# Loading wo in 1 MB pieces through the K/V ring and doing the output projection at the end of a decode kernel

## The chip, the cores and the metric

One core of one Trainium2 chip. The metric is the device time of one execution in microseconds (us). Every run told here counts as fast: none is over 1.5% above the fastest run of its kernel. The granted clock is the share of full speed at which the chip let TensorE run. Names of engines in the profile: PE is TensorE, PEld its weight loads, DVE VectorE, ACT ScalarE, POOL GpSimd, SP the engine that issues the DMAs.

## The reference

One decode step: a token (batch 2, width 1024) attends over a cache of 32 heads x 16384 keys x 128, and the result is mixed by a gate with a small MLP.

```python
q = (x @ wq).reshape(B, 1, H, Dh)                # B=2, D=1024, H=32, Dh=128
scores = einsum("bhqd,bhkd->bhqk", q, k_cache) * Dh ** -0.5   # Sk = 16384
o = einsum("bhqk,bhkd->bhqd", softmax(scores), v_cache)
a = o.reshape(B, 1, H * Dh) @ wo                 # wo: 4096 x 1024, 8 MB in bf16
out = g * a + (1 - g) * mlp(x)                   # mlp cut: layernorm, w1..w4
```

K and V are 537 MB, all weights 36 MB, everything in bf16.

## The kernel before

A planner appends operations to one queue per engine; every engine runs its queue in program order and waits on semaphores for the others. A "pair" is one (head, batch): 4 K pieces and 4 V pieces of 1 MB each, which pass through a ring of 16 slots. Odd K pieces get their scores on DVE (two products with the query, four reductions), even ones on TensorE (transposes, then matmuls with the query). V pieces follow K with a lag of 5 pieces.

```python
stream = []
for n in range(NKP):                     # 256 K pieces
    stream.append(("K", n))
    if n >= LAG:                         # LAG = 5
        stream.append(("V", n - LAG))
...
def kpath(n):                            # the last TAILP = 6 K pieces all on TensorE
    return "p" if n >= NKP - TAILP else "pd"[n % 2]

def softmax(i):                          # called once all scores of pair i are planned
    mx_tk[i] = DVE  max of the scores along the free axis
    poolmax_tk[i] = POOL partition_all_reduce(max)
    nbias_tk[i] = POOL tensor_scalar( * -scale)
    exp_tk[i] = ACT exp -> ptile, with row sums
    pooladd_tk[i] = POOL partition_all_reduce(add) of the row sums

def do_A(h):                             # output projection of one head, 8 small matmuls
    waits = [fin_tk[h * Bsz + b] for b in range(Bsz)] + [wo_loaded[h]]
    for nt_i in range(KT):               # KT = 8: 128x128 of wo against 128x2
        P.op("pe", matmul(AT_ps[...], lhsT=wor[...], rhs=otb[...]))   # AT_ps adds up over heads

def finish(i):                           # after the last V piece of pair i
    ...                                  # 1/sum on DVE; O4_ps copied to od (ACT)
    ...                                  # 4 matmuls sum od into one column; ACT scales it into otb
    if b == Bsz - 1:
        pending_A.append(h)

for (kind, n) in stream:
    if kind == "V" and b == 0 and pc == 0:       # one wo load of 256 KB per head, 3 buffers
        wo_loaded[h] = P.dma("sp", wor[...] <- A_wo[h * 128:(h + 1) * 128, :])
    ...
    if kind == "K":
        make_qrep(i), make_w(i)          # ACT copies of the query, at the pair's first K piece
        ...                              # scores, by path
        if pending_A:
            do_A(pending_A.pop(0))
    else:
        ...                              # 8 matmuls 128x4 against 128x512 per V piece, into O4_ps
```

## Time and profile before

The first three runs took 2071.6, 2074.2 and 2088.2 us.

| stage of the profiled run (2075.1 us) | us |
|---|---|
| weights and MLP, to the first K work on TensorE | 83 |
| result of the 4th pair's POOL max to that of the 62nd (58 pairs) | 1788.9, or 30.84 per pair |
| from there to the end | 88.4 |
| TensorE / DVE / DMA busy over the span | 60% / 56% / 70% |

No engine is near full, so the question is what waits for what. The page's chain that ended last, by engine:

```profile
DVE 48%; issue 34%; PE 10%; ACT 4%; POOL 2%; SPq 1%; DMA 1%; POOLq 0%; DVEq 0%
```

"issue" is time in which the chain's engine waited for nothing that the profile shows. The same chain in order of time, for one pair (start in us, duration in us, what):

```profile
1001.31 4.51 DVE prd L676 x2
...
1015.07 4.61 DVE ssb L685 x4
...
1020.18 0.37 POOL st L472
1020.55 0.06 POOLq L475 x2
...
1020.62 10.39 issue
1031.01 0.27 POOL st L475
```

Between the first and the second line lie one more round of reductions (4.61 us) and one more of products (4.50 us). DVE works through its two K pieces, takes the max, and then the chain stands for 10.39 us. The POOL all-reduce of the max over the 128 partitions (L472) starts just ahead of that; its record is 0.37 us long. Behind it POOL's sequencer runs two MODIFY_POOL_CONFIG instructions (`POOLq L475 x2`), and only 10.4 us later does the next POOL instruction start, the scaling of the max by L475.

I call the time from the start of the max's all-reduce to the start of the next POOL instruction (L475) the **POOL wait**; where the texts below speak of the all-reduce or of the POOL round trip, they mean this. After it the exp runs on ACT, then ACT's copy of the next query, then DVE again. No TensorE work is in the list.

The projection in the timeline of that same stretch (start, duration, engine, line, operation; in brackets the idle time before it and what ended it):

```profile
1040.44 0.35 PE L562 MATMUL ps<-otb,wor 128*128 128x2 bf16 x8 [0.36 <-ACT otb L593]
...
1049.78 0.28 ACT L536 ACTIVATE ssb<-ps 128x32 f32<-128x32 f32 x2 [0.52 <-PE ps L527]
...
1050.55 0.29 DVE L470 TENSOR_REDUCE st<-ssb 128x1 f32<-128x128 f32 x1
```

The eight matmuls take 0.35 us. TensorE's scores of this pair are in place at 1050.06 us, and DVE, which had its own reductions until 1050.42, starts the max at 1050.55.

The end of the timeline, from the second last exp on:

```profile
2019.49 0.40 ACT L477 ACTIVATE ptile<-ssb,st 128x128 bf16<-128x128 f32 x1 [8.31 <-POOL st L475]
...
2049.20 0.29 DVE L470 TENSOR_REDUCE st<-ssb 128x1 f32<-128x128 f32 x1 [37.53 <-ACT ssb L536]
...
2057.67 0.40 ACT L477 ACTIVATE ptile<-ssb,st 128x128 bf16<-128x128 f32 x1 [8.61 <-POOL st L475]
...
2060.49 8.87 PE L710 MATMUL ps<-ring,ptile 128*4 128x512 bf16 x32
```

29.7 us from the second last exp to the last max (here DVE waits for scores from TensorE), then the last POOL wait, then 17.4 us from the last exp to the end (2075.1), 8.9 of them the last pair's P·V.

### The profile page before, as it was taken

Reading aid. Unit: us, or ns where it says so; the run is one execution under the profiler, and the core shown is the slowest. Engines: PE = TensorE matmul, PEld = TensorE weight load, DVE = VectorE, ACT = ScalarE, POOL = GpSimd, SP = SyncE. Lnnn points to the kernel's source line nnn. Section 1 sums busy time; section 2 is a strip of 40 time slices with the busy share of each in tenths; the row PEclk is TensorE's granted clock in tenths of the full one; section 3 lists DMA queues with packets and bytes.
Section 4 is the critical chain, followed back from the end, with each engine's and each line's share of the span. In section 5 each row is a group of like instructions: output and inputs, shape, how many; then the busy total and the mean of one; then the engine's idle time right before and its main releaser. Section 6 shows DMA issues by size and latency. Waiting matters only on the chain.

```text
span 2075.1 us, 17839 instructions
## 1 busy us (share of the span) xinstructions
PE 1250.5 (60%) x7119; PEld 628.1 (30%) x7119; DVE 1166.0 (56%) x917; ACT 667.0 (32%) x1177; POOL 75.1 (4%) x213
## 2 busy tenths in 40 slices
PE   2565565665575575566566556557556656656557
PEld 2322232332232232232233223223223223323223
DVE  1365565575575566566566557557556656656620
ACT  1232233232333333333333223233333333323333
POOL 1000000000000000000000000000000000000000
PEclk9977877888888888888888888888888888778888
DMA  9996766776776776676686676677667667667650
GB/s 384 408 400 248 303 250 262 309 271 256 298 280 260 281 304 256 267 314 250 260 323 259 260 307 268 259 293 295 254 276 303 255 261 306 254 266 306 254 200 1
DMA packets 86612, 573.72 MB, mean 276 GB/s; under 512 B 9216, under 2 KB 9216, under 8 KB 19968
## 3 DMA queue, kind: packets, MB, share of 16 engines
q1 hardware_dynamic: 86528, 572.57, 70.0%
q8 instruction: 56, 0.92, 0.2%
q14 instruction: 28, 0.23, 0.0%
HBM read 572.53 MB, written 0.00 MB: 276 GB/s over the span
## 4 chain that ended last, share of the span: by engine, by line
DVE 48%; issue 34%; PE 10%; ACT 4%; POOL 2%; SPq 1%; DMA 1%; POOLq 0%; DVEq 0%
DVE ssb L685 23%; DVE prd L676 23%; PE ps L710 4%; PE ps L514 3%; ACT ptile L477 2%; PE ps L643 1%; POOL st L472 1%; SPq L242 1%; ACT ktr L653 1%; POOL st L475 1%; DVE st L470 1%; DMA ring<-in_B_w_dram 1%; PE ps L314 1%; PE ps L588 1%; ACT qrep L573 0%
## 5 line engine op out<-in xcount | busy, mean ns | idle before, releaser
L676 DVE TENSOR_TENSOR prd<-ring,qrep 128x2048 f32<-128x2048 bf16 x250 | 561.7, 2288 | 735.2 <-ACT wbuf L491 728.8
L514 PE MATMUL ps<-ktr,wbuf 128*32 128x512 bf16 x1048 | 347.8, 439 | 684.1 <-ACT ktr L653 684.1
L685 DVE TENSOR_REDUCE ssb<-prd 128x8 f32<-128x1024 f32 x500 | 574.8, 1212 | 4.3
L653 ACT ACTIVATE ktr<-ps 128x1024 bf16<-128x1024 bf16 x524 | 500.3, 1024 | 186.8 <-PE ps L643 186.4
L710 PE MATMUL ps<-ring,ptile 128*4 128x512 bf16 x2048 | 529.7, 405 | 15.3 <-ACT ptile L477 15.3
L514 PEld LDWEIGHTS ps<-ktr,wbuf 128*32 128x32 bf16 x1048 | 82.2, 99 | 812.2 <-ACT ktr L653 736.1
L643 PE MATMUL ps<-ident_f,ring 128*128 128x128 f32 x2096 | 317.6, 298 | 0.0
L643 PEld LDWEIGHTS ps<-ident_f,ring 128*128 128x128 f32 x2096 | 244.0, 150 | 115.9 <-issue 111.6
L710 PEld LDWEIGHTS ps<-ring,ptile 128*4 128x4 bf16 x2048 | 181.1, 93 | 303.8 <-issue 114.1
L477 ACT ACTIVATE ptile<-ssb,st 128x128 bf16<-128x128 f32 x64 | 25.7, 401 | 766.6 <-POOL st L475 766.6
L585 ACT ACTIVATE od<-ps 4x512 f32<-4x512 f32 x64 | 37.6, 587 | 151.7 <-PE ps L710 151.7
L588 PEld LDWEIGHTS ps<-ident_f,od 4*128 4x128 f32 x512 | 62.4, 188 | 36.3 <-ACT od L585 36.3
L588 PE MATMUL ps<-ident_f,od 4*128 4x1 f32 x512 | 67.9, 249 | 9.0 <-ACT od L585 9.0
L522 ACT ACTIVATE stsb<-ps 32x512 f32<-32x512 f32 x64 | 37.6, 587 | 104.6 <-PE ps L514 104.6
L472 POOL PARTITION_ALL_REDUCE st<-st x64 | 25.5, 399 | 901.6 <-DVE st L582 842.0
L470 DVE TENSOR_REDUCE st<-ssb 128x1 f32<-128x128 f32 x64 | 18.3, 286 | 68.3 <-ACT ssb L536 61.0
L527 PE MATMUL ps<-ident_f,stsb 32*128 32x32 f32 x256 | 27.5, 227 | 43.7 <-ACT stsb L522 43.7
L527 PEld LDWEIGHTS ps<-ident_f,stsb 32*128 32x128 f32 x256 | 20.4, 136 | 75.3 <-ACT stsb L522 75.3
L593 ACT ACTIVATE otb<-ps,st 128x1 bf16<-128x1 f32 x64 | 16.9, 264 | 80.9 <-PE ps L588 79.6
L475 POOL TENSOR_SCALAR st<-st 128x1 f32<-128x1 f32 x64 | 18.3, 286 | 661.1 <-issue 661.1
L480 POOL PARTITION_ALL_REDUCE st<-st x64 | 25.7, 401 | 389.6 <-issue 212.3
L536 ACT ACTIVATE ssb<-ps 128x32 f32<-128x32 f32 x131 | 18.6, 195 | 33.2 <-PE ps L527 33.2
(83 smaller groups left out, 172.4 us busy)
## 6 DMA issues: line engine op xcount, KB each, us to landing
ring<-in_A_k_cache_dram SPq DMA_DIRECT2D x256, 1024.0 KB, 7.2
ring<-in_A_v_cache_dram SPq DMA_DIRECT2D x256, 1024.0 KB, 7.4
ring<-in_B_w_dram SPq DMA_DIRECT2D x11, 1024.0 KB, 19.9
ring<-in_A_wq_dram SPq DMA_DIRECT2D x8, 1024.0 KB, 12.0
wor<-in_A_wo_dram SPq DMA_DIRECT2D x32, 256.0 KB, 7.5
ring<-in_B_w_dram SPq DMA_DIRECT2D x8, 896.0 KB, 15.3
x<-in_A_x_dram SPq DMA_DIRECT2D x1, 4.0 KB, 1.5
gw<-in_gate_w_dram SPq DMA_DIRECT2D x1, 2.0 KB
```

The costliest lines, as they stand in the source:

```text
L470: mx_tk[i] = P.op("dve", lambda e: e.tensor_reduce(stc(j, M_P), S_sb(j), AX.X, ALU.max), part_tk[i] + [prev(poolmax_tk, i, NPB)])
L472: poolmax_tk[i] = P.op("pool", lambda e: e.partition_all_reduce(stc(j, GMAX), stc(j, M_P), channels=128, reduce_op=RED.max), [mx_tk[i], pr ...
L475: nbias_tk[i] = P.op("pool", lambda e: e.tensor_scalar(stc(j, NBIAS), stc(j, GMAX), -scale, None, ALU.mult), [poolmax_tk[i], prev(exp_tk, ...
L477: exp_tk[i] = P.op("act", lambda e: e.activation(P_ap(j, 0, NCH), S_sb(j), ACTF.Exp, bias=stc(j, NBIAS), scale=scale, accum_out=stc(j, L_P ...
L514: e.matmul(ST_ps(i), lhsT=l, rhs=r, start=st_, stop=sp_)),
L527: tk = P.op("pe", (lambda e, t4=t4: e.transpose(Sp_ps[:, t4 * 32:(t4 + 1) * 32], stj[:, t4 * 128:(t4 + 1) * 128], ident_f[0:32, 0:32])), ( ...
L588: osum_tk[i] = P.op("pe", (lambda e, m=m: e.matmul(oT_ps, lhsT=odj[:, m * 128:(m + 1) * 128], rhs=ident_f[0:VG, m:m + 1], start=(m == 0), ...
L643: e.transpose(o, a, ident_f[:])),
L653: evac_tk[gn] = P.op("act", lambda e, o=o_pl, a=a_pl: e.activation(o, a, ACTF.Copy), ew)
L676: last = P.op(eng, (lambda e, o3=o3, i3=i3, qb3=qb3: e.tensor_tensor(o3, i3, qb3, ALU.mult)), ([ring_loaded[jp], qrep_tk[i]] + wfree) if q ...
L685: red = P.op("dve", (lambda e, o=o, a=a: e.tensor_reduce(o, a, AX.X, ALU.add)), ([last, prev(exp_tk, i, NPB)]) if g_ == 0 else ())
L710: e.matmul(O4_ps, lhsT=l, rhs=rr, start=st_, stop=sp_)),
```

## The change

The intent: take the 32 small wo loads and the 32 small projection groups out of the middle of the kernel. wo comes in 8 loads of 1 MB (4 heads each) through slots of the K/V ring near the end of the stream, and each piece is multiplied in one run of 32 matmuls. With it comes a shorter last pair: its P·V is done with V as the stationary operand (128 matmuls of one column) straight into the layout that the projection needs.

```diff
--- before.py
+++ after.py
@@ -61,7 +61,9 @@
     cfg = dict(cfg or {})
     NSLOT = cfg.get("NSLOT", 16)
     NKT = cfg.get("NKT", 4)
-    NWO = cfg.get("NWO", 3)
+    WOGAP = cfg.get("WOGAP", 2)
+    WTAIL = cfg.get("WTAIL", 2)
+    LASTBT = cfg.get("LASTBT", 1)
     NQ = cfg.get("NQ", 32)
     QKLAG = cfg.get("QKLAG", 2)
     EVAC = cfg.get("EVAC", "a")
@@ -71,6 +73,7 @@
     PSPLIT = cfg.get("PSPLIT", 4)
     NPRD2 = cfg.get("NPRD2", 2)
     TAILP = cfg.get("TAILP", 6)
+    TAILK = cfg.get("TAILK", 0)
     NT = 3
     VG = 4
 
@@ -103,7 +106,6 @@
 
     ring = nc.alloc_sbuf_tensor("ring", [128, NSLOT * PE_ELEMS], BF16)
     ktr = nc.alloc_sbuf_tensor("ktr", [128, NKT * 1024], BF16)
-    wor = nc.alloc_sbuf_tensor("wor", [128, NWO * D], BF16)
     ident_bf = nc.alloc_sbuf_tensor("ident_bf", [128, 128], BF16)
     ident_f = nc.alloc_sbuf_tensor("ident_f", [128, 128], F32)
     qsb = nc.alloc_sbuf_tensor("qsb", [128, NPAIR + NQ], BF16)
@@ -116,7 +118,7 @@
     ptile = nc.alloc_sbuf_tensor("ptile", [128, NPB * NCH], BF16)
     ssb = nc.alloc_sbuf_tensor("ssb", [128, NPB * NCH], F32)
     st = nc.alloc_sbuf_tensor("st", [128, NPB * 8], F32)
-    otb = nc.alloc_sbuf_tensor("otb", [128, 2 * Bsz], BF16)
+    otb = nc.alloc_sbuf_tensor("otb", [128, NPAIR], BF16)
     od = nc.alloc_sbuf_tensor("od", [VG, NPB * VG * 128], F32)
     prd = nc.alloc_sbuf_tensor("prd", [128, PE_ELEMS], F32)
     prd2 = (nc.alloc_sbuf_tensor("prd2", [128, NPRD2 * PE_ELEMS], F32)
@@ -177,6 +179,7 @@
     msel_ps = bank_f(1, 0, 4 * NPAIR)
     qrep_ps = bank_f(7, 0, 128)
     O4_ps = ps[0:VG, 5 * 512: 6 * 512]
+    Obt_ps = ps[:, 5 * 512: 5 * 512 + 1]
     AT_ps = bank_f(6, 0, W)
     QT_ps = bank_f(0, 0, NPAIR)
     xTp = bank_b(7, 0, W)
@@ -219,8 +222,6 @@
     P = _Plan(nc)
     slot_sem = [nc.alloc_semaphore("slot%d" % s) for s in range(NSLOT)]
     slot_uses = [0] * NSLOT
-    wo_sem = [nc.alloc_semaphore("wo%d" % s) for s in range(NWO)]
-    wo_uses = [0] * NWO
     misc_sem = nc.alloc_semaphore("misc_dma")
     misc_sem2 = nc.alloc_semaphore("misc_dma2")
     out_sem = nc.alloc_semaphore("out_dma")
@@ -409,13 +410,38 @@
         return cache[b, h, pc * PKEYS:(pc + 1) * PKEYS, :].rearrange("(p r) d -> p (r d)", p=128)
 
     NKP = NPAIR * NPC
+    HPP = max(1, min(H, PE_ELEMS // D))
+    NWOP = -(-H // HPP)
     stream = []
+    nv = 0
     for n in range(NKP):
         stream.append(("K", n))
-        if n >= LAG:
-            stream.append(("V", n - LAG))
-    for n in range(max(0, NKP - LAG), NKP):
-        stream.append(("V", n))
+        if n >= LAG and n < NKP - TAILK:
+            stream.append(("V", nv))
+            nv += 1
+    while nv < NKP:
+        stream.append(("V", nv))
+        nv += 1
+    n_tail = min(WTAIL, NWOP)
+    n_before = NWOP - n_tail
+    pos = len(stream)
+    inserts = []
+    for k_ in range(n_before):
+        pos = max(0, pos - WOGAP)
+        inserts.append(pos)
+    inserts.reverse()
+    for gw, pos in reversed(list(enumerate(inserts))):
+        stream.insert(pos, ("W", gw))
+    for gw in range(n_before, NWOP):
+        stream.append(("W", gw))
+    seen_v = set()
+    for (kind, n) in stream:
+        if kind == "V":
+            seen_v.add(n)
+        elif kind == "W":
+            need_pairs = range(n * HPP * Bsz, min(NPAIR, (n + 1) * HPP * Bsz))
+            early = [i_ for i_ in need_pairs if (i_ * NPC + NPC - 1) not in seen_v]
+            assert not early or n >= NWOP - n_tail - 1, (n, early)
 
     def kpath(n):
         if n >= NKP - TAILP:
@@ -550,20 +576,25 @@
         while len(pending_qk) > keep:
             issue_qk(pending_qk.pop(0))
 
-    def do_A(h):
-        hs = h % 2
-        s = h % NWO
-        waits = [fin_tk[h * Bsz + b] for b in range(Bsz)] + [wo_loaded[h]]
+    def wo_piece(gw):
+        h0 = gw * HPP
+        nh = min(HPP, H - h0)
+        src = A_wo[h0 * 128:(h0 + nh) * 128, :].rearrange("(t p) n -> p t n", p=128)
+        dv = (lambda s_, nh=nh: slot_ap(s_, 0, nh * D).rearrange("p (t n) -> p t n", t=nh))
+        jp, s_ = ring_dma(src, dst_view=dv)
         last = None
-        for nt_i in range(KT):
-            last = P.op("pe", (lambda e, o=AT_ps[:, nt_i * Bsz:(nt_i + 1) * Bsz],
-                               l=wor[:, s * D + nt_i * 128: s * D + (nt_i + 1) * 128],
-                               r=otb[:, hs * Bsz:(hs + 1) * Bsz], st_=(h == 0 and nt_i == 0), sp_=(h == H - 1):
-                               e.matmul(o, lhsT=l, rhs=r, start=st_, stop=sp_, skip_group_check=True)),
-                        waits if nt_i == 0 else (), track=(nt_i == KT - 1))
-        A_tk[h] = last
-
-    pending_A = []
+        for hh in range(nh):
+            h = h0 + hh
+            waits = [ring_loaded[jp]] + [fin_tk[h * Bsz + b] for b in range(Bsz)]
+            for nt_i in range(KT):
+                last = P.op("pe", (lambda e, o=AT_ps[:, nt_i * Bsz:(nt_i + 1) * Bsz],
+                                   l=slot_ap(s_, hh * D + nt_i * 128, hh * D + (nt_i + 1) * 128),
+                                   r=otb[:, h * Bsz:(h + 1) * Bsz], st_=(h == 0 and nt_i == 0), sp_=(h == H - 1):
+                                   e.matmul(o, lhsT=l, rhs=r, start=st_, stop=sp_, skip_group_check=True)),
+                            waits if nt_i == 0 else (), track=(nt_i == KT - 1))
+            A_tk[h] = last
+        ring_free[jp] = last
+
 
     def make_qrep(i):
         j = i % NPB
@@ -581,6 +612,11 @@
         hs = h % 2
         rl_tk[i] = P.op("dve", lambda e: e.reciprocal(stc(j, RL), stc(j, LSUM)),
                         [pooladd_tk[i], prev(fin_tk, i, NPB)])
+        if LASTBT and i == NPAIR - 1:
+            fin_tk[i] = P.op("act", (lambda e, o=otb[:, i:i + 1]:
+                                     e.activation(o, Obt_ps, ACTF.Copy, scale=stc(j, RL))),
+                             [pvlast_tk[i], rl_tk[i]])
+            return
         odj = od[:, j * VG * 128:(j + 1) * VG * 128]
         ocopy_tk[i] = P.op("act", lambda e: e.activation(odj, O4_ps, ACTF.Copy),
                            [pvlast_tk[i], prev(osum_tk, i, NPB)])
@@ -589,12 +625,10 @@
                 oT_ps, lhsT=odj[:, m * 128:(m + 1) * 128], rhs=ident_f[0:VG, m:m + 1],
                 start=(m == 0), stop=(m == VG - 1))),
                 ([ocopy_tk[i], t_identf] + list(b7_read)) if m == 0 else (), track=(m == VG - 1))
-        fin_tk[i] = P.op("act", (lambda e, o=otb[:, hs * Bsz + b: hs * Bsz + b + 1]:
+        fin_tk[i] = P.op("act", (lambda e, o=otb[:, i:i + 1]:
                                  e.activation(o, oT_ps, ACTF.Copy, scale=stc(j, RL))),
-                         [osum_tk[i], rl_tk[i], prev(A_tk, h, 2)])
+                         [osum_tk[i], rl_tk[i]])
         b7_read[:] = [fin_tk[i]]
-        if b == Bsz - 1:
-            pending_A.append(h)
 
     def cprime(c):
         pcq, r = c // R, c % R
@@ -605,15 +639,12 @@
         return ap.rearrange("p (r d) -> p r d", d=DH)
 
     for (kind, n) in stream:
+        if kind == "W":
+            wo_piece(n)
+            continue
         i, pc = n // NPC, n % NPC
         h, b = i // Bsz, i % Bsz
         j = i % NPB
-        if kind == "V" and b == 0 and pc == 0:
-            s = h % NWO
-            wo_uses[s] += 1
-            wo_loaded[h] = P.dma("sp", (lambda e, s=s, h=h: e.dma_start(
-                wor[:, s * D:(s + 1) * D], A_wo[h * 128:(h + 1) * 128, :])), wo_sem[s], 16 * wo_uses[s],
-                [prev(A_tk, h, NWO)])
         cache = A_k_cache if kind == "K" else A_v_cache
         jp, s = ring_dma(kv_src(cache, i, pc))
         if kind == "K":
@@ -689,14 +720,21 @@
                 else:
                     prd2_free[pb] = red
                 add_part(i, red)
-            if pending_A:
-                do_A(pending_A.pop(0))
         else:
             waits = [ring_loaded[jp]]
             if pc == 0:
                 waits += [exp_tk[i], prev(ocopy_tk, i, 1)]
             last = None
             ngq = R // VG
+            if LASTBT and i == NPAIR - 1:
+                for r in range(R):
+                    c = pc * R + r
+                    pcol = j * NCH + cprime(c)
+                    last = P.op("pe", (lambda e, l=slot_ap(s, r * DH, (r + 1) * DH),
+                                       rr=ptile[:, pcol:pcol + 1], st_=(c == 0), sp_=(c == NCH - 1):
+                                       e.matmul(Obt_ps, lhsT=l, rhs=rr, start=st_, stop=sp_)),
+                                waits if r == 0 else (), track=(r == R - 1))
+                ngq = 0
             for gq in range(ngq):
                 g_, half_ = gq // 2, gq % 2
                 is_first = (pc == 0 and gq == 0)
@@ -715,8 +753,6 @@
                 pvlast_tk[i] = last
                 finish(i)
     flush_qk(0)
-    while pending_A:
-        do_A(pending_A.pop(0))
 
     t = P.op("dve", lambda e: e.tensor_copy(aT[:], AT_ps), [A_tk[H - 1]])
     t = P.op("dve", lambda e: e.tensor_tensor(v3(gaT[:]), v3(aT[:]), bc_t(gate[:]), ALU.mult), [t, t_gate])
```

In order, the new end of the stream is (W is a wo piece, V249 the second V piece of pair 62, counted from 0, K252 to K255 and V252 to V255 the last pair): K252 W0 V247 K253 W1 V248 K254 W2 V249 K255 W3 V250 V251 W4 V252 V253 W5 V254 V255 W6 W7.

## The prediction

> **What bounds the kernel now.** After the weight phase (first 82 us) the kernel does one (head, batch) pair per 30.8 us: in the timeline, pairs 3 to 61 took 1788.9 us. The chain of waits inside one pair has no TensorE work: two DVE products (4.5 us each), two rounds of DVE reductions (4.6 us each), a max, the POOL all-reduce (10 to 11 us until the next POOL instruction starts; the chain calls it "issue"), the exp, the qrep copy, then DVE again. DVE has 48% of the chain, issue 34%, PE 10%. TensorE idles about 10 us in each pair, and DMA is at 70% (page). So DVE plus the POOL round trip bound the middle.
>
> **What the change removes, adds, moves.**
> 1. The 32 wo loads of 256 KB and the 8 matmuls after every second pair leave the middle. Such a group costs TensorE 0.35 us plus about 0.7 us of waiting for otb, in TensorE's slack, off the chain. Expected gain: about 0.
> 2. wo returns as 8 loads of 1 MB in the last ring entries, with 32 matmuls each. On TensorE four such groups sit among the last pair's K pieces, ahead of the final score matmuls; one before, one within and two after the last pair's V pieces. The weight phase's 128x2 matmuls start 27 ns apart (219 in 6.0 us), so a group is about 0.9 us, 7.2 us in all (an estimate from that).
> 3. The last pair's P·V: 32 matmuls of 512 columns (8.8 us, half of it at clock 0.5 after the POOL wait) become 128 of one column, about 3.5 us. Its copy to od (0.6 us) and four summing matmuls (1.05 us) go.
>
> **On the critical path.** From 2020 to 2048 us the chain does run on TensorE (the last six K pieces all use it), so the four groups there cost +3.7 us, less 0.3 us for the removed group. After the last exp: before, 11.3 us from the previous pair's sum (2060.5) to the last projection matmul (2071.8); after, 0.9 + 1.8 + 0.9 + 1.8 us, then about 1.8 us with the last copy hidden among them: 7 to 8 us, perhaps 9 if the clock of 0.5 slows these small matmuls. So -2 to -4 us. Tail net: about 0, -2 to +3.
>
> The final POOL wait (7.5 us where no DMA runs, 10 to 11 us where it does) should stay: by the ring's order the last wo loads land before 2040 us.
>
> In the middle one thing is unsure: pairs whose window holds a wo load and projection are 0.3 us *shorter* (30.67 against 30.97 us), with a POOL wait of 10.3 against 10.7 us. The ring also alternates halves by pair, so parity may not be the projection's doing. If it is, removing it costs up to +9 us; if the bytes under the POOL wait matter, it saves up to 10 us.
>
> The Trainium skill ("TensorE: Matmul & The Clock Gate", part 1) says an idle TensorE falls to half clock; the trace agrees (0.50 after each POOL wait). The change doesn't cure that, since the wait stays.
>
> **Predicted time:** 2072 us, 2057 to 2091 (before ranged 2071.6 to 2088.2). Chances: faster by over 2% 0.03, within 2% 0.94, slower 0.03.
>
> **What would show it.** Pair period 30.5 to 31.2 us and POOL wait 10 to 11 us as before; DVE and POOL leading the chain; four wo groups of 0.9 to 1.2 us among the last K pieces; 13 to 14 us from the last exp to the end instead of 17.4.
>
> **What would make it wrong.** The POOL wait moving by over 0.5 us in every pair; instruction supply stalls in the long runs of small matmuls at the end (the weight phase shows gaps of 1 to 3 us); wo loads landing late.

## More of the kernel before

The view of that line (`--source L475`) has them twice a pair:

```profile
L475 POOLq MODIFY_POOL_CONFIG  x128: 83/83/85, 104.4 to 2049.9; - x128
```

Such a couple stands in the trace wherever POOL goes from an all-reduce to a TENSOR_SCALAR or back. Over the 64 pairs the TENSOR_SCALAR starts 7.1 to 11.9 us behind it, and the all-reduce of the sum (L480) 5.4 to 6.6 us behind it; where two all-reduces follow each other without it, the second starts within 0.2 us of the moment at which it may. So the wait goes with the change from one kind of POOL instruction to the other. What POOL does in it the trace doesn't tell.

## The result, and the profile after

Ratios are the mean time of one kernel's fast runs over that of the other's of the same rounds, so not quite the ratio of the medians quoted beside them.

| | median us | runs | lowest to highest |
|---|---|---|---|
| before | 2084.91 | 15 | 2071.60 to 2088.44 |
| after | 2084.58 | 12 | 2076.38 to 2088.22 |

Ratio 1.0004, 95% interval 0.9984 to 1.0024: no difference. The profiled runs differ more (2075.1 against 2083.2 us), and their sum shows how a zero is made up. The boundaries are the moments at which POOL's max result of a pair was there:

| stretch | before | after | difference |
|---|---|---|---|
| start to 4th pair | 197.8 | 198.8 | +1.0 |
| 4th to 62nd pair | 1788.9 | 1794.0 | +5.0 |
| 62nd to 63rd | 32.5 | 34.8 | +2.3 |
| 63rd to 64th | 38.2 | 42.2 | +4.0 |
| 64th to the end | 17.7 | 13.5 | -4.2 |

The chain that ended last, by engine, after:

```profile
DVE 53%; issue 33%; PE 5%; ACT 3%; POOL 2%; DMA 2%; SPq 1%; DVEq 0%; POOLq 0%
```

and in order of time, one pair:

```profile
1019.62 4.61 DVE ssb L716 x4
...
1024.73 0.37 POOL st L498
...
1025.16 10.13 issue
```

The middle has the same chain with the same durations. The time from a POOL result to the next pair's start of the POOL max is 19.92 to 19.97 us in all 58 pairs after, and 19.93 us in all but a few pairs before, where it is up to 20.81. What differs from pair to pair is the POOL wait (standard deviation 0.6 us). Summed over 58 pairs, the POOL waits are 638.1 us after and 631.0 before (+7.1), and what lies above 19.93 us is 2.0 us before and less than 0.1 after (-2.0): that is the +5.0. The lead of TensorE's scores is now 0.8 to 0.9 us (median) in odd and in even pairs, so the projection had used up most of it.

The end of the timeline after:

```profile
2027.85 0.40 ACT L503 ACTIVATE ptile<-ssb,st 128x128 bf16<-128x128 f32 x1 [9.56 <-POOL st L501]
...
2032.46 1.01 PE L593 MATMUL ps<-otb,ring 128*128 128x2 bf16 x32
...
2033.40 3.58 PE L748 MATMUL ps<-ring,ptile 128*4 128x512 bf16 x8
...
2042.88 0.95 PE L593 MATMUL ps<-otb,ring 128*128 128x2 bf16 x32
...
2062.26 0.28 DVE L496 TENSOR_REDUCE st<-ssb 128x1 f32<-128x128 f32 x1 [43.48 <-ACT ssb L562]
...
2070.03 0.40 ACT L503 ACTIVATE ptile<-ssb,st 128x128 bf16<-128x128 f32 x1 [7.90 <-POOL st L501]
...
2073.72 1.84 PE L735 MATMUL ps<-ptile,ring 128*128 128x1 bf16 x64
```

Four wo groups of 0.95 to 1.01 us (two are shown) now stand between the second last exp and the last max, which are 34.4 us apart instead of 29.7. Behind the last exp the end comes after 13.2 us instead of 17.4. And the second last POOL wait has grown from 7.5 to 8.75 us: in the windows view the DMA share of the time from 2018 to 2020 us, at its start, is 1.02, since a ring with wo pieces in it is still taking in data:

```profile
2018.00:2020.00 2.00, 1.33 (x12) 1.09 (x11) 0.36 (x2) 0.28 (x3) 0.37 (x1) 1.00 1.02 328
```

(stretch, length, busy time of PE, PEld, DVE, ACT, POOL, granted clock, DMA share, GB/s). Before, the same wait began with the DMA queues empty (share 0.00 from 2008 us on). That the traffic makes the wait longer is not shown, and two traces speak against it: in e3 the same wait begins at 2006.70 us with a DMA share of 1.10 (2006 to 2008 us) and takes 7.75 us, and in e6 it begins at 1682.12 us with 0.76 (1682 to 1684 us) and takes 7.48 us. The other 1.1 us of "62nd to 63rd" stands ahead of every wo group, so I don't count it to the change: eight matmuls of a V piece took 3.2 us of the chain instead of 2.1, where the clock came back from 0.50 only 8.0 us after POOL's result instead of 5.8. In "63rd to 64th" the 4.7 us lose 0.7 to a shorter last POOL wait (7.1 against 7.8 us).

### The profile page after: what moved, and what is told of

Read it like the earlier page. It is cut to its first block, busy times and chain, and to the rows that moved or that the text cites. A ratio compares the mean times of both kernels' runs of the same rounds, so it can differ in the third digit from the quotient of the medians.

```text
span 2083.2 us, 17960 instructions
## 1 busy us (share of the span) xinstructions
PE 1243.5 (60%) x7207; PEld 626.5 (30%) x7207; DVE 1166.0 (56%) x917; ACT 666.0 (32%) x1176; POOL 74.9 (4%) x213
## 4 chain that ended last, share of the span: by engine, by line
DVE 53%; issue 33%; PE 5%; ACT 3%; POOL 2%; DMA 2%; SPq 1%; DVEq 0%; POOLq 0%
DVE ssb L716 26%; DVE prd L707 26%; PE ps L748 2%; ACT ptile L503 2%; PE ps L540 1%; SPq L243 1%; POOL st L498 1%; DMA ring<-in_A_wq_dram 1%; POOL st L501 1%; DVE st L496 1%; DMA ring<-in_B_w_dram 1%; PE ps L674 1%; PE ps L315 1%; ACT ktr L684 1%; ACT qrep L604 0%
## 5 line engine op out<-in xcount | busy, mean ns | idle before, releaser
L748 PE MATMUL ps<-ring,ptile 128*4 128x512 bf16 x2016 | 523.5, 407 | 16.2 <-ACT ptile L503 16.2
L498 POOL PARTITION_ALL_REDUCE st<-st x64 | 25.5, 398 | 906.4 <-DVE st L613 846.8
```

What stands on the lines that cost most here:

```text
L498: poolmax_tk[i] = P.op("pool", lambda e: e.partition_all_reduce(stc(j, GMAX), stc(j, M_P), channels=128, reduce_op=RED.max), [mx_tk[i], pr ...
L748: e.matmul(O4_ps, lhsT=l, rhs=rr, start=st_, stop=sp_)),
```

## The experiments

My theory: the middle is bound by DVE and the POOL wait, the projection lies off that chain, and the end trades about as much as it gains: new work on TensorE where TensorE is the chain, against a shorter last pair. Rivals: the wo loads or the 1 MB batching matter; TensorE or DMA bounds the middle; the zero comes from something else in the POOL wait.

A warning on "correct". The comparison with the reference passed every kernel below, the wrong ones as well: with these inputs the attention part is far below the rounding of the output. I therefore also ran before, after, e3, e5, e9, e10 and e11 in a functional simulation with wq, K, V and wo scaled up until the attention part was nearly all of the output (0.214 of a mean magnitude of 0.214). All seven gave the same bits, within 0.0078 of the reference; e4's kernel was off by up to 6.3. So those seven are right and e4 is wrong. Repeated in the check of this text with scales of its own, the simulation gave the same bits for e1, e2, e6, e7 and e12 too. It says nothing of time.

### e1: the last pair as it was

```diff
-    LASTBT = cfg.get("LASTBT", 1)
+    LASTBT = cfg.get("LASTBT", 0)
```

> The change with its new last pair undone (LASTBT 0: again 32 matmuls of 512 columns, the copy to od and the four summing matmuls). Theory: the tail loses what this part gained, so from the start of the last exp to the end about 20 to 21 us instead of 13.2; from the start of the second last exp to the last max as in after, about 34 us; total 7 us above after, ratio to before about 1.003. Rival (the new last pair is worth little because the POOL sum and wo bound the end): under 16 us from the last exp to the end.

Measured: 2082.02 us against 2073.95 before on that chip, ratio 1.0042 (1.0012 to 1.0072). From the last exp to the end 20.8 us, from the second last exp to the last max 34.0 us, second last POOL wait 8.5 us. As the theory says: without the new last pair the change costs, by an amount clear of noise.

### e2: the new last pair alone, on the kernel before

```diff
+            if i == NPAIR - 1:     # 32 one-column matmuls per V piece, V stationary, into Obt_ps
+                ...
+                ngq = 0
...
+        if i == NPAIR - 1:         # in finish: scale Obt_ps straight into otb
+            fin_tk[i] = P.op("act", activation(otb[...], Obt_ps, Copy, scale=1/sum), ...)
+            pending_A.append(h)
+            return
```

> The kernel before with only the new last pair added, wo as before. Theory: from the last exp to the end 10.5 to 11.5 us instead of 17.4; from the second last exp to the last max 29 to 31 us as in before; total about 6 us below before, ratio about 0.997. Rival (the wo batching is what shortens the end): 15 us or more from the last exp to the end.

Measured: 2072.48 us against 2073.95, ratio 0.9988 (0.9950 to 1.0025), so the total alone settles nothing. The trace does: 10.8 us from the last exp to the end instead of 17.4, 30.0 us from the second last exp to the last max as before (29.7). The rival falls: what shortens the end is the last pair, and wo batching has no part in it.

### e3: the wo groups where TensorE idles

```diff
-    (W pieces spread over the last twelve stream items)
+    at = stream.index(("V", NKP - NPC - 1))          # after the last score matmuls
+    stream[at:at] = [("W", gw) for gw in range(NWOP - 1)]
+    stream.append(("W", NWOP - 1))
```

> The change with seven of the eight wo groups moved on TensorE to right after the last score matmuls, where it idles for the last POOL wait. Theory: from the second last exp to the last max about 30 us (34.4 in after), from the last exp to the end 9.5 to 11 us (13.2 in after), total about 7 us below after, ratio to before about 0.997. Rival (the loads, not the matmuls, cost): the second last POOL wait grows from 8.75 us to over 10 us and eats 2 us or more of it.

Measured: 2068.96 us against 2073.95, ratio 0.9978 (0.9944 to 1.0012). Second last exp to last max 29.3 us (34.4 in after), last exp to the end 10.9 us (13.2), second last POOL wait 7.75 us. The seven groups ran as one block of 224 matmuls in 5.97 us, nearly all of it inside the last POOL wait (2044.4 to 2052.3 us):

```profile
2043.36 5.97 PE L588 MATMUL ps<-otb,ring 128*128 128x2 bf16 x224
2049.26 3.52 PE L743 MATMUL ps<-ring,ptile 128*4 128x512 bf16 x8
```

So what cost 4.7 us in after was where the matmuls stood, and the rival (the loads) falls. The edit moves the loads along with the matmuls, but the chain of after has no wait for a DMA between the second last exp and the last max. In total the gain is not clear of noise here either.

### e4: the projection eight times over

```diff
-        for nt_i in range(KT):
+        for rp_, nt_i in [(r_, n_) for r_ in range(8) for n_ in range(KT)]:
```

> The kernel before with every projection matmul issued eight times (wrong result on purpose): 56 more matmuls after every second pair, about 1.5 us each time, 47 us of TensorE in all. Theory (the projection lies in slack): in the trace the scores are ready 0.4 us before DVE needs them in pairs with a projection, so only about 1.1 us per two pairs shows, +30 to +40 us in all, ratio 1.015 to 1.02. If all of it is on the chain: +47 us or more. If TensorE has the 10 us of slack that its idle time suggests: 0.

Measured: 2144.36 us, ratio 1.0326 (1.0285 to 1.0366), about 67 us. That is above the 30 to 40 us of the theory, and taken alone it would fit the rival that had the whole projection on the chain (47 us or more). The trace tells why. The time from a POOL result to the next pair's POOL max is 19.95 us on average in pairs without a projection, as ever, and 21.96 in pairs with one, which adds up to 59.7 us over 58 pairs. Of the 29 with one, 23 lie at 20.8 to 22.1 us, 1.5 us late on average, which is about what the added matmuls take (1.4 us): next to nothing of them is hidden, since the lead in these pairs is 0.14 us (median) and not the 0.4 that I had read off one pair. The other six lie at 23.5 to 24.6. In one of these:

```profile
553.09 1.81 PE L562 MATMUL ps<-otb,wor 128*128 128x2 bf16 x64 [0.36 <-ACT otb L593]
554.83 3.58 PE L710 MATMUL ps<-ring,ptile 128*4 128x512 bf16 x8
558.34 2.67 PE L643 MATMUL ps<-ident_f,ring 128*128 128x128 f32 x12
```

The matmuls behind the small ones take 3.58 and 2.67 us; before, they took 1.89 and 1.53. The windows view has the granted clock there:

```profile
552.00:554.00 2.00, 1.64 (x43) 1.56 (x43) 1.90 (x2) 0.26 (x1) 0.00 (x0) 0.98 0.80 319
554.00:556.00 2.00, 2.00 (x37) 1.17 (x35) 2.00 (x2) 0.00 (x0) 0.00 (x0) 0.50 1.03 422
```

It fell to 0.50 at 553.9 us, in the middle of the small matmuls. The clock's record has such a fall inside the run of small matmuls in all six of these pairs and in none of the 23. Two things follow. TensorE's slack in the middle is the time by which its scores are early (0.14 us with a projection, 0.83 without), and not the 10 us that it idles: the idle time lies behind the point at which DVE takes the scores. And a run of small matmuls costs more than its own duration when the clock falls during it.

### e8: the loads kept, the projection left out

```diff
-            pending_A.append(h)
+            if h in (0, H - 1):
+                pending_A.append(h)
+            else:
+                A_tk[h] = fin_tk[i]        # wrong result on purpose
```

> The kernel before with the 32 loads kept and the projection matmuls of heads 1 to 30 left out (wrong result on purpose). Theory: without projection DVE never waits for late scores: the time from one POOL result to the next max is 19.93 us in every pair, as in after, where before has a few of 20.1 to 20.8; total within 5 us of before, ratio 0.997 to 1.001. The POOL wait's difference between odd and even pairs (10.7 against 11.1 us) stays if the loads make it and goes if the matmuls do; the mean over all pairs stays 10.8 to 11.0 us either way.

Measured: 2083.12 us against 2075.72, ratio 1.0039 (0.9997 to 1.0081): outside the 0.997 to 1.001 that I expected, though unclear. Late scores are nearly gone (0.8 us above 19.93 in total; before 2.0, e2 5.1). The POOL wait was 11.2 us in odd and 10.8 in even pairs, so the "odd pairs are shorter" that the prediction worried about is gone without the matmuls; in e4, with more of them, it was reversed too (11.15 and 10.73). The mean of all pairs was 10.99 us. Mean POOL waits of all six comparable traces: before 10.88, e2 10.84, e8 10.99 with the wo loads in the middle; after 11.00, e1 10.86, e3 10.85 without. There is no step between the groups. A tenth of a microsecond here is 6 us in the total, which is as large as all other differences; I don't know what makes the wait vary.

### e5 and e6: hide the POOL wait

If the middle is bound by DVE waiting behind the POOL wait, hiding it must move the time a lot. DVE doesn't need the max's result: it waits for ACT's copy of the next query, which is queued behind the exp, which waits for POOL. So the exp is planned later:

```diff
 def softmax(i):
     ...                                   # max, POOL max, POOL scaling as before
-    exp_tk[i] = P.op("act", exp ...)
-    pooladd_tk[i] = P.op("pool", partition_all_reduce(add) ...)
+    pending_exp.append(i)
+def flush_exp(i):                         # the two lines above, unchanged
...
     else:                                 # a V piece
         if pc == 0:
+            flush_exp(i)
             waits += [exp_tk[i], ...]
```

> The kernel before with one thing changed: the exp (and the sum behind it) is issued on ACT only just before the pair's first V piece instead of right after the max, so that ACT's qrep copy for the next pair, and with it DVE, no longer queue behind the POOL all-reduce. Theory (DVE plus the exposed POOL wait bound the middle): the pair period falls from 30.8 us to 21 to 24 us, set by DVE (18.9 us), DMA (8.4 MB, 20 to 21 us at the 415 GB/s of busy stretches) and TensorE (about 19.5 us), total 1480 to 1680 us. Rival (TensorE or DMA bounds the middle already): within 5% of before.

> The same edit on the changed kernel. Theory: the wo traffic and the projection were free only because the POOL wait left slack; with it hidden, taking them out of the middle shows. Total 0.5 to 2% below the previous run (8 to 30 us, tail cost of about 2 us included). Rival: the change is worth nothing here either, within 0.3% of the previous run.

Measured: e5 1736.07 us, ratio 0.8374 (0.8338 to 0.8410); e6 1735.64 us, ratio 0.8368 (0.8341 to 0.8395). The rival to the theory of what bounds the middle falls: the same instructions in another order on ACT and POOL save 16%. The timeline of e5 has DVE back at work during the POOL wait:

```profile
1009.58 0.37 POOL L472 PARTITION_ALL_REDUCE st<-st  x1 [6.41 <-DVE st L589]
...
1011.18 4.49 DVE L683 TENSOR_TENSOR prd<-ring,qrep 128x2048 f32<-128x2048 bf16 x2 [1.63 <-ACT wbuf L498]
...
1021.95 0.86 POOL L475 TENSOR_SCALAR st<-st 128x1 f32<-128x1 f32 x1 [11.99 <-issue]
```

The period is 25.5 us and not the 21 to 24 expected, because TensorE still waits about 5 us in each pair for the exp. And my expectation for e6 fell: with the old slack gone, the change is still worth nothing. In e5's timeline the projection stands just ahead of TensorE's wait for the exp (it ends at 1018.5 us, the exp's result comes 5.0 us later), so it is off the chain again.

### e7, e9 and e12: how far V lags behind K

```diff
-    LAG = cfg.get("LAG", 5)
+    LAG = cfg.get("LAG", 7)      # e7, with the later exp; 6 in e9, with it, and in e12, without it
```

> As e5, with V pieces two further behind K (LAG 7), so TensorE has more work between the max and the first V piece. If in e5 TensorE still waits for the exp, this falls below e5 by 1 us or more per pair (60 us); if DMA or DVE bounds e5, within 1% of it.

> As e5 with LAG 6 instead of 5. In e5 the chain ran max, POOL wait (11.8 us), exp, P.V, next scores, and TensorE still idled about 5 us in each pair before the exp; in e7 (LAG 7) the sum of one pair queued on POOL behind the max of the next and DVE waited for it. LAG 6 gives one K piece more work under the POOL wait and keeps the sum ahead of the next max. Theory: the period falls from 25.5 to 21.5 to 23.5 us, total 1480 to 1620 us. Rival (POOL's two all-reduces per pair, about 19 us with DMA traffic, or DVE's wait for the sum bound it): 25 us or more per pair, not below e5.

> The control to e9: LAG 6 alone, with the exp left where before has it. Theory (DVE queues behind the exp through ACT's order, and LAG matters only once that is gone): the chain stays DVE, POOL wait, exp, qrep, DVE; pair period 30.5 to 31.3 us, total within 1.5% of before. Rival (the larger LAG gave e9 its speed): 15% or more below before.

Measured: e7 2057.55 us, ratio 0.9933 (0.9891 to 0.9975); nearly all of e5's gain was lost, which I had not foreseen. Its chain:

```profile
1008.52 2.33 POOL st L472
...
1010.91 9.48 issue
...
1021.00 0.01 POOLq L487
1021.01 8.19 issue
1029.20 0.41 POOL st L487
...
1029.63 0.04 DVE st L589
```

At LAG 7 the plan puts the all-reduce of one pair's sum (L487) behind that of the next pair's max (L472) on POOL, and DVE, in order, waits for the sum to take its reciprocal (747 us of such waits in the list of waits). The all-reduce of the sum is again short: DVE goes on 0.43 us after its start. The 8.19 us ahead of it follow a second change on POOL (`POOLq L487`). LAG 6 puts the sum ahead of the max: e9 took 1543.49 us, ratio 0.7402 (0.7383 to 0.7422), with a period of 22.4 us, inside what I expected. e12 is the control: LAG 6 alone is slower than before, 2108.79 us, ratio 1.0104 (1.0072 to 1.0135). So the gain is the later exp's, and LAG decides only how much of it is kept.

### e10 and e11: the change and its last pair on the faster kernel

e10 is the changed kernel and e11 is e2's kernel, each with the later exp and LAG 6.

> The same on the changed kernel. If TensorE or DMA is then on the chain in the middle, the projection (0.7 us per two pairs) and the wo traffic (0.6 us per two pairs) cost the kernel before 10 to 20 us that this one does not pay: 0.4 to 1.3% below e9. If they still fall into idle time, within 0.3% of it, as e6 was of e5.

> e9 plus the new last pair alone (as e2). Theory: 5 to 8 us below e9, as e2's tail was 7 us shorter than before's. If the batching of wo is what pays once the slack is gone, it stays above e10.

Measured: e10 1547.98 us, ratio 0.7422 (0.7396 to 0.7447), against e9's 0.7402; e11 1537.99 us, ratio 0.7383 (0.7364 to 0.7403). Periods are 22.39 us in e9 and 22.42 in e10. Even at 74% of the time, with DMA 93% busy (page, DMA queues), taking wo out of the middle changes nothing there. e11 is 5.5 us below e9 by the medians, of the size expected, though the intervals overlap. It has the lowest median of all kernels run. What bounds e9's middle now (the chain has PE 44%, issue 26%, ACT 17%, POOL 8%) I did not settle.

## Why the prediction was right or wrong

- **What bounds the middle: right, and shown.** It is DVE and the POOL wait, though the wait is not the all-reduce itself, as the prediction has it (that is done 0.38 us after its start); e5 and e9, which change nothing but when the exp is planned and the lag, took 16% and 26% off, and e12 shows that the lag is not the cause.
- **The middle's gain of about 0: right in size, with a slip in the reason.** The prediction set "TensorE idles about 10 us in each pair" beside "in TensorE's slack". The slack left beside the projection is 0.14 us (median; late scores add up to 2.0 us in before, 5.1 in e2 and less than 0.1 in after), and e4 shows what happens to a projection that does not fit it, with the falls of the clock seen in six pairs: +67 us. So the change gains 2 to 5 us there, within 0.25% of the total.
- **The worry of +9 or -10 us from odd and even pairs: neither.** The mean POOL wait doesn't follow wo or projection over six traces.
- **The four groups on the chain, +3.7 less 0.3 us: measured +4.7.** The groups took 0.95 to 1.01 us as predicted (0.9 to 1.2). Their steps in the chain add 3.6 us, and the removed group takes 0.3 off. Most of the rest is clock: after the first group TensorE ran on at 0.5 until 2038 us, and the next two steps took 3.51 and 1.56 us where before had 3.00 and 0.86, which makes 1.2 us.
- **After the last exp, -2 to -4 us: measured -4.2**, the 13 to 14 us predicted being 13.2. e1 and e2 show that it is all due to the last pair: alone it takes off 6.6 us, and the wo groups without it add 3.4. No instruction supply stall showed up in the long runs of small matmuls; that worry was idle.
- **The POOL waits at the end.** The prediction spoke of the final one alone, which should stay; it took 7.1 us instead of 7.8. On the second last it said nothing, and that one grew by 1.25 us (1.0 in e1, 0.25 in e3). The cause stays open.
- **Wrong: the predicted time.** The step that failed is "Predicted time: 2072 us", for which the text's reason is only that "before ranged 2071.6 to 2088.2". It doesn't say which level of before it set out from; 2072 lies 2 us below the middle one of the three runs (2074.2). Over 15 runs before's median is 2084.91, about 11 us higher, and the change is 1.0004. Against that level 2072 is a gain of 0.6%, which isn't there. The prediction's own sum over the steps (about 0 in the middle, -2 to +3 at the end) was the better forecast: on the level of 2084.91 it gives 2083 to 2088, and after took 2084.58. What the runs showed in place of a gain: tail about +1.8 (4.7 + 1.25 - 4.2), middle -2 to -5, and a spread of several us from the POOL waits. That the parts come out so near to zero is luck as much as forecast: the groups cost 1.3 us more than predicted and the second last POOL wait 1.25 us.

The change moved work from a place where it just fitted under a longer chain to a place where half of it did not, and paid for that with a useful but separate edit to the last pair.

## What to carry to other kernels

An engine's idle time is not its slack: slack is how early its result arrives at the one that waits for it, read from two lines of the timeline. Before moving work, look for the wait on the chain that is not work at all, and ask which engine is held up only because its input is queued, in program order, behind that wait; here that was worth 16%, and 26% with a lag that suits it, and the change under study nothing. Ask also what the wait is: here it goes with the change from an all-reduce to a TENSOR_SCALAR on POOL, so scaling the max on another engine might take it off the chain; nobody ran that. And take the level of a forecast from enough runs: three runs of a kernel that varies by 0.8% don't give it to 0.5%. Nor does one group of runs give it for another: before's median was 2073.95 us in the runs of e1 to e4 (chip 2), 2075.72 in those of e5 to e8 (chip 11) and 2084.06 in those of e9 to e11 (chip 7).

## What the Trainium skill lacked or had wrong

- "TensorE: Matmul & The Clock Gate", Part 1: the page says that activity releases the throttle, and that an idle TensorE falls to half clock. The second half agrees (0.50 after the POOL waits of before and after). For the first it lacks that a stream of small matmuls without a gap need not count as activity: in e4 the clock fell from 1.00 to 0.50 inside such a stream in six pairs, and in the tail of after it stayed at 0.50 from 2072 to 2078 us with TensorE busy 2.00 us of every 2.00 on matmuls of one and two columns. When it happens is open: in e4's other 23 pairs the clock stayed at 1.00 through the stream.
- Same page, "Wait — 56ns, not 53.3ns?": "Start-to-start never drops below ≈25 ns however small N is". Agrees: 25.2 ns in e4's streams of 64 at a clock of 1.00, and 26.0 ns over e3's 224. It lacks how little the clock matters to such matmuls with a 128x128 weight load each: in after the wo groups at 1.00 start 25.4 to 25.5 ns apart and the 256 matmuls of the tail, at 0.50, 26.7 ns. (For the weight phase, also 26.7 ns, the trace of before has no clock record: its first stands at 87.9 us.)
- "GPSIMD Engine Reference", 3.2 and 4.1: these sections send partition reductions to GPSIMD and give one figure for a much larger tile. They lack that an all-reduce of a single column is done 0.38 to 0.41 us after its start in most pairs. Section 2.1, where MODIFY_POOL_CONFIG belongs, lacks that a wait comes with every change between an all-reduce and a TENSOR_SCALAR: in before 5.4 to 6.6 us towards the all-reduce, and 7.1 to 11.9 us towards the TENSOR_SCALAR. The POOL wait is 7.0 to 8.1 us in the last two pairs with no DMA traffic (all traces) and 10.9 us on average in the middle of before. What the DMA traffic does to it was not settled.
- No page: that the order in which operations are planned on ACT and POOL can be worth 16%, as in e5 (26% with LAG 6, in e9).
